# Forward D2 reshuffles on the ScalarE DMA queue, and the row stage's group tables masked by broadcast VectorE products

## The chip, the cores and the metric

One NeuronCore of a Trainium2 chip runs the kernel as one launch. The metric is the device time of a launch in microseconds, the median of several runs. TensorE (PE) multiplies; VectorE (DVE), ScalarE (ACT) and GpSimd (POOL) do elementwise work and move results out of PSUM; SyncE (SP) issues most transfers, and ScalarE can issue transfers too, between its own instructions. Each engine runs its instructions in order, and semaphores join the engines.

## The reference

The kernel computes the output and all gradients of one block in bf16: x is (1, 2048, 448), with S = 2048 and D = 448. A spectral filter is followed by a token-mixing MLP with F = 1792.

```python
def _A_ref(x, w_r, w_i):
    X = rfft2(x.astype(float32), axes=(-2, -1))
    X = X * (w_r + 1j * w_i)
    return irfft2(X, s=(S, D), axes=(-2, -1)).astype(bfloat16)

def _B_ref(x, w1, b1, w2, b2):
    h = _layernorm(x, axis=-1)
    u = _gelu(einsum("bsd,sf->bdf", h, w1) + b1)
    return (einsum("bdf,fs->bds", u, w2) + b2).transpose(0, 2, 1)

h  = x + _A_ref(_layernorm(x), A_w_r, A_w_i)
h2 = h + _B_ref(_layernorm(h), B_w1, B_b1, B_w2, B_b2)
# outputs: h2, and its vjp with grad_out for x, w_r, w_i, w1, b1, w2, b2
```

## The kernel before

The Fourier transforms are done as matrix products with tables that the kernel generates at its start. The transform over S is split in two: a *row stage*, 16 steps of short transforms together with the transform over D, and a *column stage* over 16 groups, with twiddle tables `Ut` and `Vt` of 128 x 16 x 128. Between the two the data changes its layout through eight SBUF-to-SBUF transfers into the tile `D2` (called reshuffles here, R0 to R7, one for each two rows; 226 KB each). The inverse transform goes through another set into `D3`.

**Row stage (lines 905 to 937).** In step t, `row_a(t + 1)` multiplies one folded row block by the table `Rs` (the row's 1/sigma times `Rm`, made on VectorE by `scale_R`), and its PSUM bank is moved to `blks` in `rS`. `row_b(t - 1)` multiplies these blocks by `csF`; its bank goes to `css`, a ring of four buffers. After each odd row, `row_b` puts off by 1.1 us of matmul time a transfer to `D2` (line 693), issued by SyncE. VectorE also makes the folds (`fold_prep`) and the statistics of later rows (`ln_stats`).

**Filler.** `fill(n)` takes n steps of a pending generator, so that TensorE has other products between the small ones. In the row and column stages the generator is `dg_gen`: 14 blocks of 16 matmuls of transposed W2 by grad_out. Each block's 128 x 16 x 128 transpose is a DMA transpose on SyncE (line 297, `load_w2T`) into one of five slots, three in `rE` and two in `rO`; transposes are counted from 0 to 13 here. Eight are loaded during the row stage; from the column stage's start, `fwd_x(0)` interleaves the rest with the loads of the filter's imaginary part (line 583, `w_load`, four transfers for each of the two parts, the first two of 64 and 48 partitions). `w_place` then moves the filter into its place with 16 copies on either engine. Between the last row and the column stage stands `fill(20)`.

**Group tables.** `gen_UV` (line 465) makes `Ut` and `Vt` step by step inside the row stage, up to three steps in each row, where a `yield True` ends the row's share. For each table, ScalarE computes a sine into `comp` (128 x 512), and eight products of its even or odd elements with a mask column (0 or 1 for each partition) are written to strided places of the table, 16 x 16 elements each. Each goes to the engine with the smaller estimated load.

**Who evicts.** `evac` compares two running sums of estimated cost, `load[0]` for ScalarE and `load[1]` for VectorE, and gives the eviction to the one that would be done first. PE, SP, DVE and ACT run in an order that is settled when the program is built; a change of one estimate moves later evictions from one engine to the other.

**DMA semaphores.** In the built program each transfer reports on one of eight semaphores, which are dealt out in turn over the transfers of all engines in the scheduled order. The issuing engine first waits until the previous transfer on that semaphore has landed. The first matmul of the column stage waits for all eight reshuffles.

**Last stage (lines 1407 to 1420).** `inv_rows` runs 16 rows of the inverse transform; each row takes `N_FILL_B[5]` steps of `gw_gen`, the weight-gradient products, whose evictions go to store buffers. `gx_consumer` gives each row to ScalarE, VectorE and GpSimd in small operations, and one of these goes out with each filler step. `drain()` runs what is left of the generator after the last row. `store_4` (line 1328) sends the stores of the filter-gradient of `w1`, and the last two of them from ScalarE's queue, the rest from SyncE's.

Of the kernel before, what the change touches and what calls it, by code (L numbers as in the profile page):

```python
# [10 lines left out]
BF16 = mybir.dt.bfloat16  # L11
F32 = mybir.dt.float32
I32 = mybir.dt.int32
ALU = mybir.AluOpType
ACT = mybir.ActivationFunctionType
AX = mybir.AxisListType

P = 128
# [6 lines left out]
NT = 16  # L25
# [9 lines left out]
RESH_LAG = 1.1  # L35
# [1 line left out]
SIDE = 2  # L37
CAP = 8
N_FILL_F = (6, 3, 20, 3, 24, 2)
N_FILL_B = (16, 16, 40, 8, 24, 8)  # L40
INV_SD = 1.0 / float(S * D)


# [79 lines left out]
def kernel(  # L123
# [20 lines left out]
    nc = tc.nc  # L144
    Ring.held.clear()
    load = [0.0, 0.0]
    sc = Meter(nc.scalar, load, 0)
    ve = Meter(nc.vector, load, 1)
    gp_ = nc.gpsimd
# [5 lines left out]
    mem = ctx.enter_context(tc.tile_pool(name="mem", bufs=1))  # L155
# [15 lines left out]
    def ring(reg, off, count, *dims):  # L171
        n = int(np.prod(dims))
        return Ring([cut(reg, off + i * n, *dims) for i in range(count)])
# [28 lines left out]
    def defer(us, fn, *views):  # L202
        state = [fn]

        def run():
            if state:
                state.pop()()
        later.append((clock[0] + us, len(later), run))
        later.sort(key=lambda x: x[0])
        for v in views:  # L210
            Ring.held.setdefault(id(v), []).append(run)
# [43 lines left out]
    def col(n=1):  # L255
        i = _ci[0]
        _ci[0] += n
        assert _ci[0] <= 64
        return cols[:, i:i + n]
# [145 lines left out]
    def gp_madd(out, in0, scalar, in1):  # L405
        gp_.tensor_scalar(out=gtmp, in0=in0, scalar1=scalar, scalar2=None, op0=ALU.mult)
        gp_.tensor_tensor(out=out, in0=gtmp, in1=in1, op=ALU.add)
# [45 lines left out]
    def masks(eng, c_, f_):  # L453
        msk, mk, k0, k1 = col(4), col(), col(), col()
        for j in range(4):
            eng.tensor_scalar(out=msk[:, j:j + 1], in0=f_, scalar1=float(j), scalar2=None, op0=ALU.is_equal)
        eng.tensor_tensor(out=mk, in0=msk[:, 0:1], in1=c_, op=ALU.mult)
        eng.tensor_scalar(out=k1, in0=mk, scalar1=-1.0, scalar2=1.0, op0=ALU.mult, op1=ALU.add)
        eng.tensor_tensor(out=k0, in0=mk, in1=msk[:, 0:1], op=ALU.subtract)
        eng.tensor_scalar(out=k0, in0=k0, scalar1=1.0, scalar2=None, op0=ALU.add)  # L460
        return msk, mk, k0, k1

    comp_ring = ring(rO, 0, 2, 512)

    def gen_UV():
        _, s_, c_, f_ = rows = decode(gp_)
        nrow = col()
        gp_madd(nrow, rows[0], 16.0, s_)
        msk, mk, k0, k1 = masks(gp_, c_, f_)
        slf = col()  # L470
        gp_.tensor_tensor(out=slf, in0=s_, in1=f_, op=ALU.mult)
        gp_.tensor_scalar(out=slf, in0=slf, scalar1=16.0, scalar2=1536.0, op0=ALU.mult, op1=ALU.add)
        ou, ov0, ov1, pu, pv = col(), col(), col(), col(), col()
        gp_madd(ou, c_, 1536.0, slf)
        gp_madd(ov0, c_, -512.0, slf)
        gp_.tensor_scalar(out=ov0, in0=ov0, scalar1=512.0, scalar2=None, op0=ALU.add)
        gp_.tensor_scalar(out=ov1, in0=ov0, scalar1=1024.0, scalar2=None, op0=ALU.add)
        for pt, o, kk in ((pu, ou, -1536.0), (pv, ov1, -512.0)):
            gp_.tensor_scalar(out=pt, in0=s_, scalar1=64.0, scalar2=kk, op0=ALU.mult, op1=ALU.add)
            gp_madd(pt, pt, mk, o)  # L480
        yield
        ve.tensor_scalar(out=permI[:], in0=krow[:, 0:P], scalar1=nrow, scalar2=None, op0=ALU.is_equal)
        ve.scalar_tensor_tensor(out=base[:, 0, :, 1], in0=fix, scalar=mk, in1=base[:, 0, :, 1], op0=ALU.mult, op1=ALU.add)
        for dst, o0, o1, pt in ((Ut, ou, ou, pu), (Vt, ov0, ov1, pv)):
            t = ftmp(1024 if dst is Ut else 2048, 16, 16, 2).bitcast(I32)
            for k, o in ((0, o0), (1, o1)):
                ve.tensor_scalar(out=t[:, :, :, k], in0=base[:, :, :, k], scalar1=s_, scalar2=o,
                                 op0=ALU.mult, op1=ALU.add)
                yield
            ve.tensor_scalar(out=t[:, 0, :, 1], in0=base[:, 0, :, 1], scalar1=s_, scalar2=pt, op0=ALU.mult, op1=ALU.add)  # L490
            ve.tensor_scalar(out=t, in0=t, scalar1=2047, scalar2=None, op0=ALU.bitwise_and)
            yield
            yield True
            comp = comp_ring.next()
            sc.activation(out=comp, in_=t.rearrange("p g l c -> p (g l c)"), func=ACT.Sin, scale=s2048, bias=half_uv)
            yield True
            cv = comp.rearrange("p (g l c) -> p g l c", g=16, l=16)
            for c, k in ((1, k0), (0, k1)):
                ve.tensor_scalar(out=cv[:, 0, :, c], in0=cv[:, 0, :, c], scalar1=k, scalar2=None, op0=ALU.mult)
            yield  # L500
            d0 = dst[:, :, 0:64].rearrange("p g (l f) -> p g l f", f=4)
            d1 = dst[:, :, 64:112].rearrange("p g (l f) -> p g l f", f=3)
            for j in range(4):
                m = msk[:, j:j + 1]
                dj = d1[:, :, :, j - 1] if j else dst[:, :, 112:128]
                for o, c in ((d0[:, :, :, j], 0), (dj, 1)):
                    if load[1] + 0.24 < load[0] + 0.38:
                        ve.tensor_scalar(out=o, in0=cv[:, :, :, c], scalar1=m, scalar2=None, op0=ALU.mult)
                    else:
                        sc.activation(out=o, in_=cv[:, :, :, c], func=ACT.Copy, scale=m)  # L510
                    yield
    Rp = rO[:, 1536:1536 + P]

    def gen_RT():
# [87 lines left out]
    D2 = cut(r2, 0, NG, 2, KW)  # L602
# [4 lines left out]

    _ei = [0]

    def resh_eng():  # L610
        _ei[0] += 1
        return nc.sync

    def rowbase(s_):
        return 32 * (s_ // 4) + s_ % 4
# [54 lines left out]
    def row_b(h, quarters=False):  # L670
        u, c = divmod(h, 2)
        if u < 0 or u >= NT // 2:
            return
        pd = ps_ff()
        pv = pd[:, 0:452].rearrange("p (c k) -> p c k", c=2)
        pq = pd[:, 0:452].rearrange("p (c e k) -> p c e k", c=2, e=2)
        for w in (1, 0):
            for b in range(2):
                if quarters:
                    mm(pq[:, 1 - w, b, :], lhsT=blks[u][0:DC, 2 * (2 * w + b) + c].rearrange('p j x -> p (j x)'),  # L680
                       rhs=csB[0:DC, w, b, 0:KW // 2], start=True, stop=True)
                    continue
                mm(pv[:, 1 - w, :], lhsT=blks[u][0:DC, 2 * (2 * w + b) + c].rearrange('p j x -> p (j x)'), rhs=csF[0:DC, w, b, :],
                   start=(b == 0), stop=(b == 1))
        if c == 0:
            css[u] = cs_ring.next()
        cs = css[u]
        if quarters:
            evac(out=cs[:, c].rearrange("p w (j e) -> p w e j", e=2), in_=pq)
        else:  # L690
            evac(out=cs[:, c], in_=pv)
        if c:
            defer(RESH_LAG, lambda: nc.sync.dma_start(out=D2[u:u + 121:8].rearrange("p g c k -> p (g c k)"),
                                                      in_=cs.rearrange("p x c k -> p (x c k)")), cs)

    def s2_stage(get_x, on_mult, ml, n_fill, gap, make_inv, after_fwd=None, scale=None):
# [203 lines left out]
    for c in range(2):  # L900
        sc.copy(out=Rp.rearrange("p (a q b c) -> p c a q b", c=2, q=8, a=4)[:, c],
                in_=Rm[:, 64 * c:64 * c + 64].rearrange("p (q a b) -> p a q b", q=8, a=4))
    FILL_A = (3, 3, 3, 3, 3, 3, 3, 3, 3, 3, 3, 3, 3, 3, 3, 3)
    FILL_B = (3, 3, 3, 3, 3, 3, 3, 3, 3, 3, 3, 3, 3, 3, 3, 3)
    for t in range(NT):
# [11 lines left out]
        if t == NT - 1:  # L917
            row_b(t)
# [7 lines left out]
        if t in GROUPS:  # L926
            a, b = GROUPS[t]
# [232 lines left out]
    for ch in range(2):  # L1160
        ve.tensor_scalar(out=csI[0:KC, :, ch, :], in0=csI[0:KC, :, ch, :], scalar1=halves[0:KC, ch:ch + 1], scalar2=None,
                         op0=ALU.mult)
# [120 lines left out]
    o4 = out_4.rearrange("(p t) f -> p t f", t=NT)  # L1283
# [41 lines left out]
                            out(pv, w, c + 1, i)  # L1325
                        yield

    def store_4(t, a, n, o):
        eng = nc.scalar if t >= NT - 2 and a else nc.sync
        eng.dma_start(out=o4[:, t, a:a + n], in_=o[:, 0:n])  # L1330

    pending.append(gw_gen(NFB, lambda c, k, a, b: goT[a:b, k, c * 512:(c + 1) * 512], S,
                          lambda j, a, n, o: nc.sync.dma_start(out=out_6[j * P:(j + 1) * P, a:a + n], in_=o[:, 0:n]), ost))
    pending.append(gw_gen(NT, lambda c, k, a, b: du_t[c][a:b, :, k, :], F,
                          store_4,
                          Ring(ring(rG, 0, 8, S // 2).views + ost.views), NFB // 2))
    load_W(3)
    for t in range(NT - LAG, NT + 2):
# [9 lines left out]
    for i in range(2):  # L1348
        gen_neg(UTn[:, 8 * i:8 * i + 8, :], UTt[:, 8 * i:8 * i + 8, :])
    fill(N_FILL_B[2])  # L1350
    Meter.slack = 4.0
    s2_stage(bwd_x, bwd_mult, 0, N_FILL_B[3], N_FILL_B[4], False, {5: lambda: load_du(0), 9: lambda: load_du(1), 13: lambda: load_du(2)}, 2.0 * INV_SD)
    Meter.slack = 2.0
# [57 lines left out]

    inv_rows(gx_consumer, N_FILL_B[5], aT_ring, (), True)
    while held_ops:
# [36 lines left out]
```

## Time and profile before

| | |
|---|---|
| runs | 359.11, 358.55, 359.77 us (median 359.11) |
| profiled execution | 359.11 us, its span 357.2 us |
| busy of the span: PE, ACT, DVE, POOL | 96%, 60%, 71%, 19% |
| transfers: bytes moved, mean rate | 81.62 MB, 229 GB/s |
| granted TensorE clock, mean | 0.987 |

The span is the time from the first to the last instruction that the profiler saw; the launch's own time is 1.9 us longer. Times below count from the start of the span. The busy share of TensorE is that of pipelined matmuls whose ends are modelled, so a full slice says that TensorE was not waiting, and no more. The chain that ended last is mostly TensorE's own:

```profile
PE 79%; ACT 7%; DVE 6%; DMA 4%; issue 2%; SPq 1%; POOL 0%; ACTq 0%; DVEq 0%
PE ps_mm L218 66%; PE ps_ff L218 13%; DMA rO<-in_B_w_dram 2%; ACT rO L82 2%; DVE stats L82 2%; ACT rG L82 1%; DMA rA<-in_A_x_dram 1%; DVE r L82 1%; ACT Ut L82 1%; DVE rA L82 1%; DVE rS L82 1%; SPq L297 1%; ACT Vt L82 1%; ACT rX L82 0%; ACT rS L82 0%
```

Nearly all elementwise work has line 82 and nearly all matmuls line 218, since helpers record them; tiles tell them apart: `rS` holds the row stage's blocks, `r` several buffers (`css` and `D2` among them), `rX` the column stage's results.

### The profile page before, as it was taken

How to read it: one execution, taken by the hardware profiler on the slowest of the kernel's cores; microseconds unless marked ns; L12 is line 12 of the kernel's file. 1: busy time of each engine (PE TensorE's matmuls, PEld its weight loads, DVE VectorE, ACT ScalarE, POOL GpSimd, SP SyncE). 2: the span in 40 equal slices, each digit the busy share in tenths (PEclk: the TensorE clock that was granted, in tenths of full speed). 3: DMA queues.
4: the chain of work that ended last, by engine and by line, in shares of the span. 5: the costliest groups of instructions: out<-in, count | busy, mean ns of one | idle time of the engine just before them, and what ended most of it. 6: DMA issues, size and time to landing. Idle time of an engine off the chain costs nothing.

```text
span 357.2 us, 6450 instructions
## 1 busy us (share of the span) xinstructions
PE 341.5 (96%) x2133; PEld 183.8 (51%) x2133; DVE 252.5 (71%) x679; ACT 213.8 (60%) x457; POOL 67.7 (19%) x227
## 2 busy tenths in 40 slices
PE   6898998899999999999999999999999999999994
PEld 2455665555645555555555555544444444455641
DVE  5897626992884888775226978784498766499994
ACT  4669836965986545504221355565477776588883
POOL 8667000000220000001001111110000000056771
PEclk9699999999999999999999999999999999999998
DMA  8999999847999999997886999999976878999996
GB/s 207 287 200 234 200 198 162 169 140 252 280 292 336 302 348 241 252 246 218 194 192 134 192 210 194 221 175 264 264 214 201 238 196 236 245 215 221 247 286 234
DMA packets 147672, 81.62 MB, mean 229 GB/s; under 512 B 95480, under 2 KB 139768, under 8 KB 147384
## 3 DMA queue, kind: packets, MB, share of 16 engines
q1 hardware_dynamic: 147352, 80.83, 94.7%
q8 instruction: 16, 0.26, 0.3%
q10 hardware_dynamic: 288, 0.39, 0.3%
q14 instruction: 16, 0.13, 0.1%
HBM read 27.56 MB, written 23.89 MB: 144 GB/s over the span
## 4 chain that ended last, share of the span: by engine, by line
PE 79%; ACT 7%; DVE 6%; DMA 4%; issue 2%; SPq 1%; POOL 0%; ACTq 0%; DVEq 0%
PE ps_mm L218 66%; PE ps_ff L218 13%; DMA rO<-in_B_w_dram 2%; ACT rO L82 2%; DVE stats L82 2%; ACT rG L82 1%; DMA rA<-in_A_x_dram 1%; DVE r L82 1%; ACT Ut L82 1%; DVE rA L82 1%; DVE rS L82 1%; SPq L297 1%; ACT Vt L82 1%; ACT rX L82 0%; ACT rS L82 0%
## 5 line engine op out<-in xcount | busy, mean ns | idle before, releaser
L218 PEld LDWEIGHTS <-r 128*128 128x128 bf16 (+2 forms) x660 | 61.7, 104 | 49.6 <-issue 2.7
L218 PEld LDWEIGHTS <-rS 128*128 128x128 bf16 (+2 forms) x496 | 40.5, 99 | 38.3 <-issue 7.0
L218 PE MATMUL ps_mm<-rD,r 128*128 128x448 bf16 x224 | 44.5, 352 | 0.0
L82 ACT CAST rO<-ps_mm 128x512 bf16<-128x512 f32 (+1 forms) x62 | 33.5, 583 | 13.8 <-PE ps_mm L218 11.1
L218 PE MATMUL ps_mm<-rC,rE 128*128 128x448 bf16 x144 | 36.0, 369 | 3.3 <-DMA rC<-in_grad_out_dram 3.3
L218 PEld LDWEIGHTS <-rst 128*128 128x128 bf16 (+1 forms) x320 | 23.8, 97 | 29.3 <-issue 13.5
L82 ACT CAST r<-ps_ff 128x452 bf16<-128x452 f32 x58 | 33.4, 576 | 8.8 <-PE ps_ff L218 8.4
L218 PE MATMUL ps_mm<-r,rst 128*128 128x512 bf16 (+3 forms) x192 | 36.4, 353 | 0.0
L218 PE MATMUL ps_mm<-rB,r 128*128 128x448 bf16 x160 | 31.2, 352 | 0.1
L218 PE MATMUL ps_mm<-rG,rst 128*128 128x512 bf16 (+1 forms) x128 | 28.2, 380 | 0.0
L82 ACT ACTIVATE r<-ps_mm,rstd_h 128x448 bf16<-128x448 f32 x16 | 10.1, 633 | 26.1 <-PE ps_mm L218 26.1
L82 ACT ACTIVATE r<-rC 128x448 bf16<-128x448 bf16 x16 | 9.1, 572 | 26.8 <-DMA out_dram<-r 12.9
L82 DVE SCALAR_TENSOR_TENSOR r<-ps_mm,b2col,r 128x448 bf16<-128x448 f32 x16 | 10.9, 682 | 19.9 <-PE ps_mm L218 17.9
L82 DVE CAST rO<-ps_mm 128x512 bf16<-128x512 f32 (+1 forms) x18 | 11.8, 658 | 15.2 <-PE ps_mm L218 14.3
L82 ACT ACTIVATE rG<-rG 128x896 bf16<-128x896 bf16 x14 | 13.3, 950 | 14.9 <-DVE rG L82 14.6
L218 PEld LDWEIGHTS <-rO 128*128 128x128 bf16 (+1 forms) x165 | 15.6, 98 | 12.2 <-DMA rO<-in_B_w_dram 1.8
L218 PE MATMUL ps_mm<-rE,rS 128*128 128x448 bf16 x112 | 21.5, 352 | 0.0
L82 ACT CAST rG<-ps_mm 128x512 bf16<-128x512 f32 (+1 forms) x33 | 16.6, 541 | 7.3 <-PE ps_mm L218 7.2
L1180 POOL TENSOR_SCALAR lcol<-lcol 128x1 f32<-128x1 f32 x16 | 8.5, 530 | 65.1 <-ACT r L82 65.1
L218 PE MATMUL ps_mm<-rC,rO 128*128 128x448 bf16 x80 | 19.1, 352 | 1.5 <-DMA rO<-in_B_w_dram 1.5
L1371 POOL TENSOR_SCALAR lcol<-lcol 128x1 f32<-128x1 f32 x16 | 5.5, 342 | 78.5 <-ACT r L82 78.5
L218 PEld LDWEIGHTS <-rE 128*128 128x128 bf16 x148 | 14.4, 101 | 11.3 <-issue 5.0
(198 smaller groups left out, 662.6 us busy)
## 6 DMA issues: line engine op xcount, KB each, us to landing
out_dram<-rO SPq DMA_DIRECT2D x34, 256.0 KB
r<-in_B_w_dram SPq DMA_DIRECT2D x5, 1024.0 KB
r<-r SPq DMA_DIRECT2D x16, 226.0 KB
r<-r SPq DMA_DIRECT2D x32, 113.0 KB
rS<-in_B_w_dram SPq DMA_DIRECT2D x4, 896.0 KB
out_dram<-rG SPq DMA_DIRECT2D x10, 256.0 KB
rO<-in_B_w_dram SPq DMA_DIRECT2D x2, 1024.0 KB
w_d<-rG SPq DMA_DIRECT2D x1, 1808.0 KB
```

The costliest lines, as they stand in the source:

```text
L82: fn(**kw)
L218: nc.tensor.matmul(out, lhsT=lhsT, rhs=rhs, start=start, stop=stop)
L297: nc.sync.dma_start_transpose(out=wT, in_=B_w2[j * P:(j + 1) * P, :].rearrange("f (t c) -> f t c", c=P))
L1180: gp_.tensor_scalar(out=m1, in0=ms, scalar1=-1.0 / D, scalar2=None, op0=ALU.mult)
L1371: gp_.tensor_scalar(out=m1, in0=ms, scalar1=-2.0 / D, scalar2=None, op0=ALU.mult)
```

## The change

Four things differ.

1. The reshuffles of the forward pass are issued by ScalarE. The backward pass (`quarters`) keeps SyncE. At each issue 0.55 us is added to ScalarE's estimated load.
2. In `gen_UV`, seven of the eight mask products of each table become two products on VectorE: one of 16 x 16 x 4 and one of 16 x 16 x 3 elements a partition, whose second operand is the mask row in bf16 (`mskb`, copied once by GpSimd), repeated over groups and lanes, while the first operand repeats each sine over the masks. Each ends the row's share of `gen_UV` (`yield True`). The eighth goes to either engine by the load sums (`evac_mask`).
3. The last stage takes 9 filler steps in each row, not 8.
4. All stores of the filter gradient leave from SyncE's queue.

```diff
-N_FILL_B = (16, 16, 40, 8, 24, 8)
+N_FILL_B = (16, 16, 40, 8, 24, 9)
...
+    mskb = mem.tile([P, 1, 1, 4], BF16, name="mskb")
+
+    def evac_mask(out, in_, m):
+        if load[1] + 0.43 < load[0] + 0.7:
+            ve.tensor_scalar(out=out, in0=in_, scalar1=m, scalar2=None, op0=ALU.mult)
+        else:
+            load[0] += 0.3
+            sc.activation(out=out, in_=in_, func=ACT.Copy, scale=m)
...
         msk, mk, k0, k1 = masks(gp_, c_, f_)
+        gp_.tensor_copy(out=mskb[:, 0, 0, :], in_=msk)
...
-            for j in range(4):
-                m = msk[:, j:j + 1]
-                dj = d1[:, :, :, j - 1] if j else dst[:, :, 112:128]
-                for o, c in ((d0[:, :, :, j], 0), (dj, 1)):
-                    if load[1] + 0.24 < load[0] + 0.38:
-                        ve.tensor_scalar(out=o, in0=cv[:, :, :, c], scalar1=m, scalar2=None, op0=ALU.mult)
-                    else:
-                        sc.activation(out=o, in_=cv[:, :, :, c], func=ACT.Copy, scale=m)
-                    yield
+            for out, c, j in ((d0, 0, 0), (d1, 1, 1)):
+                n = 4 - j
+                load[1] += 0.06 + 256.0 * n / 960.0
+                nc.vector.tensor_tensor(out=out, in0=cv[:, :, :, c:c + 1].broadcast_to([P, 16, 16, n]),
+                                        in1=mskb[:, 0:1, 0:1, j:4].broadcast_to([P, 16, 16, n]), op=ALU.mult)
+                yield True
+            evac_mask(dst[:, :, 112:128], cv[:, :, :, 1], msk[:, 0:1])
+            yield
...
-    def resh_eng():
-        _ei[0] += 1
-        return nc.sync
+    def resh_eng(on_act=True):
+        if not on_act:
+            return nc.sync
+        load[0] += 0.55
+        return nc.scalar
...
-            defer(RESH_LAG, lambda: nc.sync.dma_start(out=D2[u:u + 121:8].rearrange("p g c k -> p (g c k)"),
+            defer(RESH_LAG, lambda: resh_eng(not quarters).dma_start(out=D2[u:u + 121:8].rearrange("p g c k -> p (g c k)"),
                                                       in_=cs.rearrange("p x c k -> p (x c k)")), cs)
...
-    def store_4(t, a, n, o):
-        eng = nc.scalar if t >= NT - 2 and a else nc.sync
-        eng.dma_start(out=o4[:, t, a:a + n], in_=o[:, 0:n])
-
...
-                          store_4,
+                          lambda t, a, n, o: nc.sync.dma_start(out=o4[:, t, a:a + n], in_=o[:, 0:n]),
```

In the program that the changed kernel builds to, the loads of the filter and the transposes follow each other on SyncE without the reshuffles between them, and the eight semaphores are dealt out anew: R0 to R7 share theirs with, in this order, transpose 1, the last load of x, the load of b1, transpose 5, R2, R3, R4 and the first load of the imaginary filter.

## The prediction

> **What bounds the kernel now.** I read the slices first, then the waits of TensorE, then the queues in the stretch where they fall. The two rows below are TensorE's busy tenths and the mean share of the 16 DMA engines, in 40 slices of 8.9 us.
>
> ```profile
> PE   6898998899999999999999999999999999999994
> DMA  8999999847999999997886999999976878999996
> ```
>
> TensorE is full from slice 13 (107 us) to the tail, so only the first 105 us and the last 7 hold time to win; there the DMA engines are as full. The list of TensorE's waits (total, times, longest) has three of weight:
>
> ```profile
> PE ps_ff L218 <- ACT rS L82: 1.6, 1, 1.6
> PE ps_mm L218 <- DMA rO<-in_B_w_dram: 1.5, 1, 1.5
> PE ps_ff L218 <- ACT rX L82: 0.9, 1, 0.9
> ```
>
> The timeline puts them at 28.4, 59.15 and 67.7 us. The first is the row stage: ScalarE works on the group tables while row 7's bank, complete at 26.1, waits for its eviction.
>
> ```profile
> 27.64 1.93 ACT L82 ACTIVATE Ut<-rO,cols 128x256 bf16<-128x256 bf16 x3
> 29.30 0.69 ACT L82 CAST rS<-ps_ff 128x512 bf16<-128x512 f32 x1
> ```
>
> The second is a late W2 transpose, number 9 of 14 (counted from 0). SyncE's queue shows why:
>
> ```profile
> 37.62 1.05 SPq L583 DMA_DIRECT2D rB<-in_A_w_r_dram  x2
> 41.59 5.57 SPq L693 DMA_DIRECT2D r<-r  x3
> 47.25 2.24 SPq L297 DMA_TRANSPOSE rO<-in_B_w_dram  x1
> 49.55 2.35 SPq L583 DMA_DIRECT2D rB<-in_A_w_i_dram  x4
> 52.00 5.02 SPq L297 DMA_TRANSPOSE rO<-in_B_w_dram  x1
> ```
>
> From 38.7 to 47.2 SyncE stands before the last three D2 reshuffles, which wait for evictions, and transpose 8, the four loads of the imaginary filter and transpose 9 stand behind them. The trace's semaphore updates give the landings: reshuffles R0 to R7 at 31.50, 34.51, 38.06, 39.27, 45.08, 47.94, 48.67, 50.01; transpose 8 at 51.95; the first imaginary load (64 partitions) at 54.58; transpose 9 at 60.61. The column stage's first matmul, which needs all of D2, starts at 50.31, without a stall but only 0.3 us after R7.
>
> How much those reshuffles held up shows in the DMA share, the column after the granted clock:
>
> ```profile
> 27.00:41.00 14.00, 12.38 (x103) 8.27 (x102) 10.35 (x35) 12.67 (x25) 6.72 (x30) 1.00 1.13 233
> 41.00:47.00 6.00, 5.96 (x48) 4.08 (x47) 3.39 (x8) 3.63 (x8) 0.11 (x1) 1.00 0.97 154
> 47.00:50.00 3.00, 3.00 (x18) 1.56 (x16) 0.23 (x1) 0.53 (x1) 0.00 (x0) 1.00 0.64 139
> ```
>
> Saturated, the engines read 1.13; before R7 lands they have slack.
>
> **The masks.** Sixteen products go, 11 on ScalarE and 5 on VectorE; in come four broadcast products on VectorE (128x1024 and 128x768 twice) and two 128x256 products, which the order of the changed program puts on ScalarE.
>
> ```profile
> L82 ACT ACTIVATE Ut<-rO,cols 128x256 bf16<-128x256 bf16 x6 | 3.9, 771 | 0.5 <-DVE rO L82 0.5
> L82 DVE TENSOR_SCALAR Vt<-rO,cols 128x256 bf16<-128x256 bf16 x3 | 1.0, 451 | 0.0
> ```
>
> ScalarE: 3.9 + 3.0 (the Vt group) = 6.9 us for 11, 0.63 each in a run; 9 fewer are 5.6 us less. VectorE: three strided products took 0.99 us end to end, 0.33 each for 256 columns, so 1024 cost at most 4 x 0.33 = 1.32 and 768 0.99. The dense 128x904 product, 0.624 us, is the other bound: 0.71 and 0.53. Operands and output are strided here, so I take near the upper end, 1.15 and 0.9: 4.1 us for both tables, less 5 x 0.33 = 1.65 gone, +2.5 us. Laid into VectorE's row from 25.6 us (rescale, fold, statistics in order), they finish the fold for rows 8 and 9 at 27.5, when row 8 starts (27.48), and the fold for rows 10 and 11 0.1 to 0.2 us late. Row 7's eviction moves from 29.3 to about 26.9. So this part takes 1.3 to 1.6 us off the row stage. [...]
>
> **The reshuffles.** Eight issues move from SyncE (0.53 to 0.70 us each) to ScalarE, +4.5 us there against 5.6 gone. Each also waits: every transfer reports on one of eight semaphores dealt out in turn over both queues, and waits until the previous user has landed. In the changed program R7 takes the semaphore of the first imaginary load: ScalarE may not issue R7 before that load lands. In the kernel before its predecessor was R3, landed at 39.27. Behind R7 on ScalarE stand the eviction of transpose 6's product and the column stage's evictions; TensorE's first column matmul waits for R7 itself.
>
> So: when does that load land? SyncE, freed, issues transposes 6 and 7, the four real loads, transpose 8 (free once block 3 is consumed, 34.3) and the load at about 37.5, but the engines are full. Counted from 54.58 where it landed before: R6 and R7 no longer go ahead of it, 2 x 1.25 (the spacing of R1 after transpose 6, 1.22, and of R2 after transpose 7, 1.27) = 2.5; the slack is filled, 6 x (1 - 0.97/1.13) + 3 x (1 - 0.64/1.13) = 0.85 + 1.3 = 2.15. That gives 49.9; without the slack 52.1; with the idle 0.6 us at 25 to 26 (share 0.41) filled as well 49.3. R7 would be ready at 45.2 to 46.6. It loses 3 to 5 us.
>
> From the start of its issue R7 took 3.38 us before (46.63 to 50.01). Bounds: 1.94 for a store on an idle queue (351.47 to 353.41), 8.1 for R4 behind two filter loads. On its own queue I take 3.4: landing at 53.3, first column matmul 0.3 later, 53.6 against 50.31: **+3.3 us**. TensorE has nothing but the 20 fill matmuls (4.35 us) to cover this, and those cover R7's old latency. The row stage's 1.5 us vanish into the same wait: it ends by a DMA, not by TensorE.
>
> In return transpose 9, issued about 43.5 and behind some 6 us of loads after 49.9, lands near 57; it is wanted 9.1 us after the column stage starts, at 62.7. Its **1.5 us** wait goes. The 0.9 us wait for the rX eviction stays: ScalarE's order there still has three, then two filter placements (0.95 us each) ahead of it, and two more earlier. Bounds on this: 0.9 won, 0.9 lost.
>
> [...] If R7's 1.3 us of transfer then take turns with the filter loads, it lands 1.3 us later and the sum grows by that; if the own queue is as good as an empty one, the sum is as above.
>
> **The tail.** The fill per row goes from 8 to 9 in the last stage: 16 yields, some 18 matmuls, leave the drain of 46 (7.94 us). TensorE's total is unchanged and it is full from 250 to 345, so its end stays. VectorE needs 2.17 us a row; the row pitch grows from about 2.27 to 2.45, so it stops lagging, but its last row comes 16 x 0.2 = 3.2 us later and ends near 352.7 (was 351.44). The last two stores on SyncE instead of ScalarE: before, the four last ones were issued at 351.90 to 352.90 and landed at 355.79, with the DMA share at 1.0 from 352.5 to 355; bytes decide, not the issuer. After, two of the four no longer stand behind the last out_1 store. I take 0, bounds -0.5 and +0.6.
>
> **Sum.** 359.11 (the profiled execution, which is also the median; span 357.2) + 3.3 - 1.5 = **360.9 us**. With landing 49.3 to 52.1, flight 1.94 to 5 and the tail, it runs from 358.4 to 364; its own likely range is 359.9 to 362.7.
>
> **Rivals.** (a) The wait on the semaphore is short: the load lands by 46, or R7 is later than I think. Then TensorE keeps 1.4 of the row stage and the 1.5: 359.1 - 2.9 = **356.2**, faster. For it: two queues may keep the engines busier than one. Against it: 4.6 us of transfers (transpose 8, the load: 50.01 to 54.58) that ran after R7 now run before it, on engines at 1.13. It decides if R7 lands before about 49. (b) The gate costs what it frees: R7 lands at 51.5 to 52, **359.1**, within 0.3% (about what this kernel's measurement can tell from no change). For it: the slack could be larger than the share says. (c) R7, sharing with filter loads, takes as long as R4, 8.1 us: column stage at 58.3, +8 - 1.5, **365.6**. Against: R4 stood behind those loads in one queue. (d) VectorE, 98% busy from 20 to 30, becomes the row stage's bound; hidden behind the gate if there is one, else (a) loses 0.3 to 1.
>
> **Chances.** Forecast 0.62, (a) with (d) 0.14, (b) 0.18, (c) 0.06. Faster by over 0.3% 0.14, same 0.18, slower 0.68. The range, 358.3 to 363.3, reaches over (b) and leaves out (c) and most of (a).
>
> **What would show it.** After: no wait of TensorE on an rS eviction near 28; ScalarE standing before its last reshuffle from about 46 to 50; a TensorE wait of some 4 us ahead of the first Vt matmul against D2, ended by a DMA; no wait for rO near 60; VectorE's broadcast products 1.1 and 0.9 us long; the last row product later and the last store landing as far after TensorE's end as before (3.6 us). If TensorE enters the column stage before 50, the gate was not there and I am wrong in sign.

## The result, and the profile after

The changed kernel takes 371.09 us (median of 4 runs, 370.57 to 374.07) against 359.12 for the kernel before on the same chip: 1.035 times as long, 95% interval 1.0292 to 1.0408. The forecast was 360.9 us in a range of 358.3 to 363.3. The sign was right and the place was right, but the loss is 12.0 us where 1.8 were expected.

The slices of the page show the place. TensorE, the granted clock, and the mean share of the DMA engines:

```profile
PE   5897960989999999999999999999999999999994
PEclk9798995799999999999999999999999999999998
DMA  8999999633699999999686999997967669999996
```

The span is now 371.9 us, so a slice is 9.3 us long. Counted from 0, slice 5 (46.5 to 55.8 us) is six tenths busy and slice 6 is empty, just where the column stage used to begin; the clock is low in slices 6 and 7. The list of TensorE's waits (total, times, longest) has one new row that carries nearly everything:

```profile
PE ps_ff L218 <- DMA rO<-in_B_w_dram: 12.0, 1, 12.0
PE ps_mm L218 <- DMA rO<-in_B_w_dram: 2.3, 1, 2.3
PE ps_ff L218 <- ACT rX L82: 1.2, 1, 1.2
```

The first row is the wait before the first matmul against `D2`, which starts at 64.65 us (50.31 before). The profile puts it down to the transfer that ended last by its records, a W2 transpose into `rO`; the matmul needs the last reshuffle R7, which landed at 64.52. The second row is another wait, in the row stage: it ends at 30.19, with the landing of transpose 3 at 30.14, and e8, a second profile of the same kernel, does not have it. The row stage's wait for the rS eviction is gone, as forecast, and so is the wait near 60 for transpose 9. ScalarE's timeline (start, us, engine, line, operation) shows where R7 stood:

```profile
49.54 8.52 ACTq L704 DMA_DIRECT2D r<-r  x2
58.09 0.53 ACT L82 CAST rD<-ps_mm 128x448 bf16<-128x448 f32 x1 [10.80 <-DMA rB<-in_A_w_i_dram]
```

R6 and R7 are issued in this group: R6 at 49.54, right after R4, whose semaphore it shares, had landed at 49.46, and R7 only at 57.51, right after the first imaginary load landed at 57.44. And SyncE, which used to stand before R5 to R7, has run ahead:

```profile
38.19 2.47 SPq L592 DMA_DIRECT2D rB<-in_A_w_r_dram  x4
40.76 8.35 SPq L297 DMA_TRANSPOSE rO<-in_B_w_dram  x1
49.16 2.86 SPq L592 DMA_DIRECT2D rB<-in_A_w_i_dram  x4
52.12 8.94 SPq L297 DMA_TRANSPOSE rO<-in_B_w_dram  x1
```

The issue of transposes 8 and 9 and of the imaginary loads begins before R7's. Transpose 8 took 2.24 us to issue before and takes 8.35 now, transpose 9 took 5.02 and takes 8.94; why, no run here isolates. From 14.3 us at the column stage's start to the end little changes: TensorE's last matmul ends 14.6 us later than before (366.82 against 352.21), the span 14.7.

The profiled run (374.07) was the longest of its four. In e8 the column stage starts at 59.34; the sizes of single terms are read from it.

### The profile page after: what moved, and what is told of

The parts are those of the page before. It is cut to its first block, busy times and chain, and to the rows that moved or that the text cites. A ratio compares the mean times of both kernels' runs of the same rounds, so it can differ in the third digit from the quotient of the medians.

```text
span 371.9 us, 6446 instructions
## 1 busy us (share of the span) xinstructions
PE 343.6 (92%) x2133; PEld 184.9 (50%) x2133; DVE 255.0 (69%) x675; ACT 211.3 (57%) x451; POOL 66.9 (18%) x228
## 4 chain that ended last, share of the span: by engine, by line
PE 76%; DMA 7%; DVE 6%; ACT 5%; issue 2%; SPq 1%; POOL 0%; ACTq 0%; DVEq 0%
PE ps_mm L218 63%; PE ps_ff L218 13%; DMA rO<-in_B_w_dram 6%; DVE r L82 3%; ACT rO L82 2%; ACT rG L82 1%; DMA rA<-in_A_x_dram 1%; DVE stats L82 1%; SPq L297 1%; DVE rA L82 1%; ACT r L82 0%; ACT rX L82 0%; DVE rG L82 0%; DVE rX L82 0%; DVE rS L82 0%
## 5 line engine op out<-in xcount | busy, mean ns | idle before, releaser
L218 PE MATMUL ps_mm<-rC,rE 128*128 128x448 bf16 x144 | 37.5, 379 | 3.2 <-DMA rC<-in_grad_out_dram 2.3
L82 ACT CAST r<-ps_ff 128x452 bf16<-128x452 f32 x56 | 32.3, 577 | 11.5 <-PE ps_ff L218 11.3
L218 PE MATMUL ps_ff<-r,Vt 128*128 128x452 bf16 x32 | 11.8, 367 | 13.2 <-DMA rO<-in_B_w_dram 12.0
L218 PE MATMUL ps_mm<-rC,rO 128*128 128x448 bf16 x80 | 20.1, 370 | 2.3 <-DMA rO<-in_B_w_dram 2.3
L82 DVE CAST rO<-ps_mm 128x512 bf16<-128x512 f32 x17 | 11.6, 689 | 15.3 <-PE ps_mm L218 14.5
L82 ACT ACTIVATE rG<-rG 128x896 bf16<-128x896 bf16 x14 | 13.3, 950 | 14.9 <-DVE rG L82 14.7
L218 PEld LDWEIGHTS <-rE 128*128 128x128 bf16 x148 | 14.5, 103 | 12.3 <-issue 5.1
L1191 POOL TENSOR_SCALAR lcol<-lcol 128x1 f32<-128x1 f32 x16 | 8.5, 531 | 65.1 <-ACT r L82 65.1
```

The lines of the kernel that those rows point to most:

```text
L82: fn(**kw)
L218: nc.tensor.matmul(out, lhsT=lhsT, rhs=rhs, start=start, stop=stop)
L1191: gp_.tensor_scalar(out=m1, in0=ms, scalar1=-1.0 / D, scalar2=None, op0=ALU.mult)
```

## The experiments

The candidates after the first profile were: A, two queues in flight at once slow each other; B (later G), the semaphore that R7 shares with the first imaginary load is a gate and the gate is the loss; C, the other parts carry some of it. Theory O, that what matters is only what has been issued ahead of the reshuffles, came out of e9 below. Each ratio is to runs of the kernel before made together with that experiment (medians from 359.12 to 360.25 us).

**e1: the reshuffles back on SyncE, all else of the change kept.**

```
-resh_eng(not quarters).dma_start(out=D2[...
+resh_eng(False).dma_start(out=D2[...
```

> The changed kernel with its eight forward D2 reshuffles back on SyncE's queue; masks by broadcast products, the fill of 9 and the two stores on SyncE stay. Theory A (two queues in flight at once slow each other's transfers) and theory B (only the shared-semaphore gate of the last reshuffle costs) both say that all of the +12 us goes with the queue: first column matmul at 48.7 to 50.3 us, the TensorE wait on the rS eviction near 28 gone, transpose 9 as late as before (1.5 us): 357.5 to 359.3 us. Theory C (the masks, the fill or the stores carry a good part of it) says 363 or more.

Measured 359.06 us, 0.9998 [0.9982, 1.0014] of before. C falls: masks, fill and stores together are worth nothing that can be told. The first column matmul starts at 49.74, 0.57 earlier than before.

**e2: the reshuffles on ScalarE, nothing else changed from before.**

```
-    nc.sync.dma_start(out=D2[...
+    (nc.sync if quarters else resh_eng()).dma_start(out=D2[...
...
     def resh_eng():
-        _ei[0] += 1
-        return nc.sync
+        load[0] += 0.55
+        return nc.scalar
```

> The kernel before with nothing changed but the queue: the eight forward reshuffles leave from ScalarE. The last reshuffle again has the first imaginary load as its predecessor on the semaphore. Theory A: first column matmul at 62 to 66 us, transposes of SyncE 5 to 9 us each to issue, 369 to 373 us. Theory B: the gate is there but the load lands near 50 to 52 without the masks' help, 360 to 364 us. Theory C: 359 to 361 us.

Measured 366.71, 1.0212 [1.0185, 1.0238]: the queue alone loses 7.6 us, between the expectations of A and B. The first imaginary load landed at 52.61, R7 was issued at 52.71 and landed at 58.42; column stage from 58.55. The gate is there, and R7's flight of 5.7 us comes on top.

**e5: the imaginary loads asked for one step later, so R7 follows R3 on its semaphore.**

```
-            for kind in "TWWWWTTT":
+            for kind in "TTTT":
...
+        if c2 == 1:
+            for _ in range(4):
+                next(w_loads)
```

> The changed kernel with the four imaginary-filter loads asked for one step of the column stage later, so that transposes 9 to 13 go ahead of them on SyncE and the last reshuffle's predecessor on its semaphore becomes reshuffle R3 (landed at 41.7 in the changed kernel). Theory A: flights stay at 6 to 12 us, R6 and R7 land at 55 to 60, first column matmul there, 364 to 368 us. Theory B (the gate alone): first column matmul at 50 to 52, 358 to 361 us.

Measured 368.06, 1.0261 [1.0215, 1.0308]. R7 was issued at 46.15 and the column stage began at 53.28, 11 us before the first profile of the changed kernel but still 3.0 after the kernel before: R7 took 6.9 us and landed 0.2 us before transpose 9, which SyncE had issued ahead of it. The time is not won. The span of e5 is 7.6 us longer than before: 3.0 are this start, some 2.7 the half clock that follows the idle time before it (5.4 us of it), 3.3 more us of waits for rX (4.2 for 0.9; the imaginary loads now land at 64 to 68), less the 1.5 us wait for transpose 9, which goes.

**e7 and e11: R7 alone moved, to SyncE and to ScalarE.**

```
e7:  +resh_eng(not quarters and u != 7).dma_start(out=D2[...
e11: +resh_eng(not quarters and u == 7).dma_start(out=D2[...
```

> The changed kernel with one reshuffle of eight, the last (R7), back on SyncE's queue. On its semaphore R7 then follows the first real-filter load, landed long before; SyncE again stands before R7 and issues transpose 8 and the imaginary loads behind it. Theory B (the gate: what costs is R7 held until the imaginary load has landed): nearly all of the +12 us goes, first column matmul at 50 to 52, 358 to 361 us. Theory A (copies of a second queue and SyncE's transposes slow each other): R0 to R6 still take 6 to 12 us, R6 lands after 54, first column matmul at 55 or later, 363 us or more.

> The mirror image: only R7 leaves from ScalarE, R0 to R6 from SyncE. Its predecessor on the semaphore is the first real-filter load, so there is no gate, but transpose 8 and the imaginary loads are issued by SyncE without waiting for R7 and share the engines with it. Theory B: R7 is issued at 46 to 47 as before, lands at 50 to 53, first column matmul there, 357 to 361 us. Theory A: R7's flight grows to 6 us or more, first column matmul at 53 to 56, 361 to 364 us.

e7: 358.97, 0.9994 [0.9965, 1.0022], column stage at 49.97. Seven of eight reshuffles on the second queue cost nothing, so A in its plain form falls. e11: 361.0, 1.001 [0.9981, 1.0038]; no gate, but transpose 8 was issued (44.51) before R7 (46.17), R7 took 6.0 us, and the column stage began at 52.24, 1.9 late. The time hardly shows it, because transpose 9 is then no longer waited for (1.5 us).

**e8: the changed kernel again.**

> The changed kernel once more, for a second profile, since the first one was of a run 3 us above the others. If the late stretch of the first profile (transpose 7 landing at 42.6, R3 at 41.7) belongs to that run alone, the first column matmul is at 60 to 62 and the time at 370.5 to 371.5; if it belongs to the kernel, it stays at 64 to 65.

Measured 370.94 in the profiled run and 367.91, on average 9.3 over the kernel before of the same group. The column stage starts at 59.34, so 5 us of the first profile's 64.65 belong to that run. The stretches of e8 (length, then busy time and instructions of TensorE, its weight loads, VectorE, ScalarE and GpSimd; then granted clock, DMA share, GB/s):

```profile
40.00:50.00 10.00, 9.98 (x73) 6.31 (x73) 4.97 (x11) 2.27 (x4) 0.11 (x1) 1.00 1.13 177
50.00:59.30 9.30, 0.00 (x0) 0.00 (x0) 0.00 (x0) 1.02 (x2) 0.00 (x0) 0.74 1.15 186
59.30:62.00 2.70, 2.66 (x10) 1.41 (x11) 0.63 (x1) 0.00 (x0) 0.00 (x0) 0.50 1.07 231
62.00:65.00 3.00, 3.00 (x17) 1.91 (x16) 0.63 (x1) 1.82 (x6) 0.11 (x1) 0.54 0.44 99
```

TensorE does nothing for 9.3 us while the DMA share reads 1.15, and the column stage then begins at half clock.

**e9: the reshuffles on GpSimd's queue, which shares no semaphore with SyncE's transfers.**

```
+(nc.sync if quarters else nc.gpsimd).dma_start(out=D2[...
```

> The changed kernel with the eight reshuffles on GpSimd's queue in place of ScalarE's: no reshuffle shares a semaphore with SyncE's transfers, so no gate, but again two queues in flight at once, and SyncE runs ahead to the imaginary loads. Theory B: first column matmul at 50 to 54, 358 to 363 us (GpSimd's own issue time is not known from any row and may add to it). Theory A: flights of 6 to 12 us stay, first column matmul at 56 to 62, 364 to 370 us.

Measured 368.69, 1.0233 [1.0176, 1.0289], column stage at 59.56. Without any gate R7 left at 48.22 and landed at 59.43, 11.2 us later and 0.2 us before transpose 9 (59.62). B fails here. Either GpSimd's queue is slow by itself, or what SyncE had put on the engines stands in front of the reshuffles whatever their own queue is: theory O.

**e12: all reshuffles on ScalarE, but SyncE held.** A 32-byte copy on SyncE reads R7's buffer, so SyncE stands before it until R7's data is there.

```
+            if u == 7 and not quarters:
+                defer(RESH_LAG, lambda: nc.sync.dma_start(out=hold, in_=cs[0:1, 1, 1, 0:16]), cs)
```

> The changed kernel, all eight reshuffles on ScalarE's queue, with one 32-byte copy added on SyncE that reads the last reshuffle's buffer: SyncE stands before it until that buffer is evicted, as it stood before R5 to R7 in the kernel before, and issues transpose 8 and the imaginary loads only then. On its semaphore R7 then follows the first real-filter load. Theory O (what costs is that SyncE, freed, runs ahead and its transpose 8, imaginary loads and transpose 9 stand in front of the reshuffles on the shared engines): first column matmul at 49.5 to 51.5, 358 to 360.5 us. Theory A (reshuffles on a second queue are slow in themselves): R4 to R7 take 6 us or more, first column matmul at 54 or later, 363 us or more.

SyncE's timeline of e12; `hold` is the small copy:

```profile
45.77 0.57 SPq L708 DMA_DIRECT2D hold<-r  x1
46.44 2.52 SPq L297 DMA_TRANSPOSE rO<-in_B_w_dram  x1
49.02 2.32 SPq L593 DMA_DIRECT2D rB<-in_A_w_i_dram  x4
```

R7, issued on ScalarE at 45.77, lands at 49.61 (3.8 us), and the column stage starts at 49.74, as in e1, with all eight on the second queue. In this profile (a run of 359.83) the whole loss is gone. Its ten runs spread from 359.2 to 365.1, for a reason that this profile doesn't show: their median is 362.95, above the 358 to 360.5 that O expected, and the ratio 1.0036 [0.9999, 1.0073] is that of the seven shortest, without three of 364.8 to 365.1. So e12 shows the cause by its times of landing and start; as a cure it is less sure than e7.

**e3 and e4: after and before with plain copies in place of the transposes.** Transposes were suspected (theory T), since reshuffles kept landing 0.1 to 0.3 us before one. Each W2 block is copied untransposed in 256-byte pieces; what is computed from it is not the reference's.

```
-        nc.sync.dma_start_transpose(out=wT, in_=B_w2[j * P:(j + 1) * P, :].rearrange("f (t c) -> f t c", c=P))
+        rows = B_w2[j * P:(j + 1) * P, :].rearrange("f (t c) -> (f t) c", c=P)
+        nc.sync.dma_start(out=wT, in_=rows.rearrange("(t p) c -> p t c", p=P))
```

> The changed kernel with its 14 W2 transposes replaced by plain copies of the same bytes in 256-byte pieces (the filter-gradient inputs come out untransposed, so part of the output is not the reference's). To be read against e4_before_plain. Theory T (a reshuffle of the second queue lands only as the transpose in flight on SyncE's queue ends, 0.1 to 0.3 us before it, and this is a property of transposes): without transposes R0 to R6 take 2 to 4 us, and e3 stands 2 to 6 us over e4. Theory O (any bytes issued ahead have the same effect): flights of 4 to 10 us stay, and e3 stands 8 to 12 us over e4.

> The kernel before with the same replacement of its 14 transposes by plain copies. Under every theory the order on SyncE's one queue stays, so 357 to 361 us if such copies move as fast as transposes; it is the base for e3_after_plain.

e4: 358.25, 0.9937 [0.9916, 0.9959]; e3: 372.72, 1.035 [1.0292, 1.0408], 14.5 us over e4, with the column stage at 62.00 against 48.88. In e3 the reshuffles R4 to R7 take 7.6 to 10.3 us from issue to landing, where T expected 2 to 4 of R0 to R6, so the loss does not need transposes. The gap of 14.5 us is larger than the 8 to 12 that was expected of O, and cannot be read as O's alone, because another gate is in it: R4 shares its semaphore with a real-filter load that landed at 43.48, and ScalarE stood before R4 until then, with evictions behind it (ScalarE's timeline, then TensorE's wait for them):

```profile
43.58 0.54 ACTq L705 DMA_DIRECT2D r<-r  x1
44.16 0.54 ACT L82 CAST r<-ps_ff 128x452 bf16<-128x452 f32 x1 [9.71 <-DMA rB<-in_A_w_r_dram]
```

```profile
PE ps_ff L218 <- ACT r L82: 8.0, 1, 8.0
```

**e13: e1 with transpose 9 asked for before the imaginary loads.**

```
-            for kind in "TWWWWTTT":
+            for kind in "TTWWWWTT":
```

> e1_resh_sync (masks by broadcast, everything on SyncE's queue) with transpose 9 asked for before the four imaginary loads in place of after them. If order on the shared engines is what sets these times, transpose 9 lands at 55 to 56 in place of 60.4, TensorE's wait for it (1.9 us in e1) goes, and the imaginary loads land some 2.5 us later (60), which the filter placements may or may not feel: 357.0 to 358.0 us if not, 358.5 to 359.5 if so.

Measured 359.38 where before took 360.21 over the runs it is compared with: 0.9969 [0.9943, 0.9994]. Transpose 9 lands at 54.61, TensorE no longer waits for it, the imaginary loads end at 60.29 (57.45 in e1). It has the lowest ratio of the kernels that compute the reference, but 0.3% is about what can be told from nothing and 1.9 us of wait won are hardly seen in the time.

**e6 and e15: gate and bytes apart.** In e6 the smallest imaginary piece goes out before transpose 8; this turns the semaphores by one, so that R7 follows R4 and R6 follows transpose 8. R7 then has no gate of its own, but it stands behind R6 on ScalarE, and R6 waits for transpose 8. In e15 (one queue, like e1) transpose 8, the imaginary loads and transpose 9 are asked for before R6 and R7.

```
e6:  +        for c_, d, ps in ((0, A_w_r, parts), (1, A_w_i, parts[3:]), (1, A_w_i, parts[:3])):
     +        for _ in range((9, 10, 11, 12, 12).count(t)):
     +            for kind in "TWWWTTT":
...
e15: +        if t == 13:
     +            for kind in "TWWWWT":
...
     +            for kind in "TT":
```

> The changed kernel with the smallest piece of the imaginary filter (16 partitions of 225 numbers) asked for before transpose 8 in place of last. This turns the semaphores by one: R7 follows R4, R6 follows transpose 8, R5 the last real-filter piece; none follows an imaginary load of any size. All reshuffles stay on ScalarE and SyncE runs ahead as in the changed kernel. Theory G (the semaphore of the imaginary load holds R7, and that wait is the loss): R7 can leave when transpose 8 has landed, 50 to 51.5, takes 3.4 and the first column matmul is at 54 to 55.5, 362 to 365 us. Theory O (the bytes that SyncE has issued ahead are the loss, with or without the semaphore): R7 lands with transpose 9, first column matmul at 58 to 60, 367 to 371 us.

> e1_resh_sync (masks by broadcast, everything on SyncE's queue, 359.06) with transpose 8, the four imaginary loads and transpose 9 asked for before R6 and R7 in place of after them: no second queue, and no reshuffle on the semaphore of a load that is still under way. Theory O: the same bytes stand ahead of R6 and R7, so R7 lands at 55 to 60 and the column stage starts there: 362 to 369 us. Theory A or G (the second queue itself, or its semaphore): neither is there, so 358.5 to 361 us.

e6: 371.07, 1.0295 [1.0226, 1.0363]. R6 left at 50.28, after transpose 8 had landed at 50.20; R7 left at 50.93, its own semaphore free since 49.27, and landed at 59.49, 8.6 us later; column stage at 59.63, where the gated kernel has 59.34. A gate of the kind seen in e3 costs TensorE 2.6 us of the row stage here (R4, held until transpose 7 landed at 40.14), so the time of e6 is not that of a kernel without gates; R7's landing is what it tells. e15: 369.91, 1.0264 [1.0213, 1.0315], with neither a second queue nor such a semaphore. SyncE's timeline of e15, the reshuffles last but one:

```profile
40.41 7.63 SPq L297 DMA_TRANSPOSE rO<-in_B_w_dram  x1
48.10 2.35 SPq L592 DMA_DIRECT2D rB<-in_A_w_i_dram  x4
50.55 5.00 SPq L297 DMA_TRANSPOSE rO<-in_B_w_dram  x1
55.65 1.27 SPq L704 DMA_DIRECT2D r<-r  x2
57.02 5.54 SPq L297 DMA_TRANSPOSE rE<-in_B_w_dram  x2
```

and the row of its TensorE waits (total, times, longest):

```profile
PE ps_ff L218 <- issue: 10.2, 1, 10.2
```

R7 lands at 59.86 and the column stage starts at 60.07. The profile names no releaser for this wait, but the first matmul starts 0.2 us after R7's landing; in the other runs of the table below it is 0.04 to 0.2.

The column stage's start thus follows one thing, what SyncE has issued ahead of R7:

| kernel | ahead of R7 | R7 issued, landed | column stage | ratio to before |
|---|---|---|---|---|
| e12 (ScalarE, SyncE held) | nothing new | 45.77, 49.61 | 49.74 | 1.0036 |
| e7 (R7 on SyncE) | nothing new | 46.18, 49.83 | 49.97 | 0.9994 |
| e11 (R7 on ScalarE) | transpose 8 | 46.17, 52.20 | 52.24 | 1.001 |
| e5 (no gate) | transposes 8, 9 | 46.15, 53.08 | 53.28 | 1.0261 |
| e8 (gate) | transposes 8, 9, imaginary loads | 53.60, 59.20 | 59.34 | 1.0268 |
| e6 (R7 behind R6, no gate of its own) | the same | 50.93, 59.49 | 59.63 | 1.0295 |
| e9 (GpSimd, no gate) | the same | 48.22, 59.43 | 59.56 | 1.0233 |
| e15 (one queue) | the same | 56.36, 59.86 | 60.07 | 1.0264 |

The last four differ in queue and gate, leave R7 over a range of 8 us, and land it within 0.7. e2, with the old masks, is like e8: 52.71, 58.42 and 58.55. The ratios of e5 and e6 hold other losses too, as said above, and that of e12 leaves out its three longest runs.

## Why the prediction was right in sign and wrong in size

**The masks.** Right in the products and in the wait, too high in the gain. The broadcast products took 1.22 and 0.93 us for 1.15 and 0.9 (VectorE's timeline of the changed kernel):

```profile
25.45 1.22 DVE L516 TENSOR_TENSOR Ut<-rO,mskb 128x1024 bf16<-128x1024 bf16 x1
28.11 0.93 DVE L516 TENSOR_TENSOR Ut<-rO,mskb 128x768 bf16<-128x768 bf16 x1
```

The 1.6 us wait for the rS eviction went, and the gain vanished before the column stage. e1 shows how small it is even without the second queue: where 1.3 to 1.6 us were forecast for the row stage, R7 is issued 0.84 us earlier (45.79 for 46.63), lands 0.40 earlier, and transpose 9's wait takes 0.4 back:

```profile
PE ps_mm L218 <- DMA rO<-in_B_w_dram: 1.9, 1, 1.9
```

**The gate.** Its existence, place and order were right: R7 left 0.07 us after the first imaginary load landed (0.08 in e8). But the forecast made it the cause, and e6 and e9 show that it is only another form of the wait: without it R7 leaves 2.7 us (e6) and 5.4 us (e9) sooner than in e8 and lands 0.2 to 0.3 later. The forecast also priced this one gate alone: R6 waited for R4 (issued at 45.53 in e8, R4 landed at 45.45), for which its sum has no term.

**The failing step: the load's landing, 49.9 us.** In e8 it was 53.52, 3.6 late and beyond the bounds of 49.3 to 52.1. The forecast took 54.58 and drew 2.15 us from "the slack is filled", reading the DMA share as a rate: 1.13 full, 0.97 and 0.64 free. The share is the time that packets were under way, not bytes: it reads 1.13 at 233 GB/s in the forecast's own first row and 1.15 at 186 in e8. The kernel before, over the same stretch as e8's first row above:

```profile
40.00:50.00 10.00, 9.96 (x73) 6.26 (x71) 4.52 (x11) 5.17 (x11) 0.11 (x1) 1.00 0.90 157
```

157 GB/s x 10 us are 1.57 MB, against 1.77 MB in e8. A share a quarter higher moved 0.20 MB more, 1.1 us at the 186 GB/s of the next stretch. The other 2.5 us, for R6 and R7 no longer standing ahead of it, are not there in full either: the load lands 1.1 earlier than before for both terms together, in e8 (53.52) as in e15 (53.45), where both reshuffles come after it on one queue.

**The second failing term: R7's flight, 3.4 us "on its own queue".** It was 5.6 in e8 (7.0 in the first profile), and 8.6 in e6. The queue was its own, the way was not: transpose 9, whose issue ran from 47.56 to 56.13 in e8, landed at 59.45, 0.25 after R7. R7 did not move slowly, it waited. These are the packets, MB and share by queue from 53.95 to 57.4 us and from 57.4 to 58.3 in e8; q1 is SyncE's queue and q10 ScalarE's, whose one packet in the first stretch has 4 bytes:

```profile
q1 hardware_dynamic: 1968, 0.58, 121.5%
q10 hardware_dynamic: 1, 0.00, 0.1%
```

```profile
q10 hardware_dynamic: 144, 0.23, 83.6%
q1 hardware_dynamic: 188, 0.04, 31.3%
```

The whole of R7 passes in 0.8 us, from 3.9 us after its issue on. A transpose is 2048 packets of 256 bytes here, so the trace lets one count when its last packet starts: 57.45 for transpose 9 in e8, and R7's first packet starts at 57.45. It is 56.67 and 56.67 in e2, 62.87 and 62.88 in the first profile, 50.34 and 50.34 for transpose 8 and R7 in e11, and in e6 56.58 for transpose 9 and for R6, which R7 follows. In these five cases the reshuffle on ScalarE's queue thus went when the transpose that SyncE had begun ahead of it was through, and no earlier; whether it stood at the engines or before them, the trace does not tell.

The forecast had this transpose in its sum, but only as a gain for TensorE later, and not as bytes in front of R7; rival (c), R7 as slow as R4 behind loads, was set aside because "R4 stood behind those loads in one queue". e15 and e6 show that one queue or two makes no difference there.

That transfers of two queues stand in each other's way is what the runs show (the column stage starts at 59.34 in e8, on two queues, and at 60.07 in e15, on one), and the forecast, which weighed it at 1.3 us, should have let it decide. That the queues take turns, on which that 1.3 us rested, was the author's assumption. In the five cases just shown ScalarE's queue took none. Elsewhere there are some: R5's packets start from 49.87 to 54.05 in the first profile, among those of transpose 8, whose last starts at 53.87, and on GpSimd's queue in e9 R7's run from 54.76 to 58.73, where transpose 9's last starts at 57.94, and it still lands at 59.43. Nor is the late landing a matter of what comes after the packets: R7 lands 0.95 us after its last packet ends in e8 (58.25, 59.20) and 0.99 in e12 (48.62, 49.61), where it lands early.

**The rivals.** (a) fell: R7 did not land before 49. What (b) described, a late start paid for by transpose 9's wait, is e11: +1.9 and -1.5. (d) was small: in e1 TensorE's waits for VectorE between 20 and 75 us are 0.8 us in all, where they were 0.5.

**The clock, a term that was missing.** After the idle stretch of e8 the clock is 0.50 for 2.7 us and 0.54 for 3.0. TensorE's work went by it: on the chain that ended last three filler matmuls take 1.12 us at 60.25 and 0.57 at 65.83. That makes an estimate of 2.7 x 0.50 + 3.0 x 0.46 = 2.7 us.

**The sum again.** In e8: start of the column stage +9.0 (3.6 + 2.2 more than the +3.3 forecast), clock +2.7, transpose 9's wait gone -1.5, makes +10.2; the last matmul with `Vt` of the backward pass's column stage indeed starts 10.2 later (302.39 for 292.15). The tail, taken as 0 with bounds of -0.5 and +0.6, is at the upper bound or over it: the last store lands 3.58 us after TensorE's last matmul before, 4.18 in the changed kernel, 4.25 in e1, 5.23 in e8. With it the span of e8 is 11.7 longer (TensorE's end 10.5). In e1 it eats what the masks brought: TensorE ends 0.3 us earlier, the span 0.1.

e2 loses 7.6 us and the full change 12.0 (9.3 in e8's two runs), though their column stages start at 58.55 and 59.34. Of the 3.7 us between the spans of the two profiles, 365.2 and 368.9, the tail makes 1.6 (3.59 against 5.23), the start 0.8 and the shorter half clock some 0.6 (4.3 us against 5.4); the rest was not taken apart.

Two things stay open. Of the 5.3 us by which the first profile was later than e8 at the column stage's start, 2.7 are there when the row stage ends, after the wait at 30.19 and the half clock that followed it; from 22 to 30 us the transfers ran at 108 GB/s there and at 213 in e8, and why is not shown. And the spread of e12 has no cause shown.

## What to carry to other kernels

An engine that stands before a late transfer is also holding back everything queued behind it, as SyncE did in the kernel before until 47.2 us. Before moving that transfer to another queue, list what the first queue will issue instead, and price the moved transfer as landing after what has been issued ahead of it, whatever queue it is on (here R7 landed at 59.20 to 59.86 from three different queues). If the transfer is urgent, keep the hold (leave the last urgent transfer on the busy queue, as in e7, or make the queue wait for its data, as in e12, whose times spread), and read free DMA capacity from bytes, not from the busy share (1.13 stood beside 177 GB/s in e8 and beside 233 in the kernel before).

## What the runs showed of the hardware

TensorE's granted clock was halved after idle stretches far shorter than the long waits, but not after each of them. After an idle of 2.2 us (e11) the granted clock stayed at 1.00; after 3.8 us (e5) it was 0.50 at the restart. These are the first stretches of the column stage in each:

```profile
52.20:54.00 1.80, 1.76 (x12) 1.12 (x13) 0.63 (x1) 0.21 (x1) 0.00 (x0) 1.00 1.29 252
```

```profile
53.20:55.00 1.80, 1.72 (x6) 0.88 (x7) 0.63 (x1) 0.00 (x0) 0.00 (x0) 0.50 1.21 274
```

The same 1.8 us hold 12 matmuls in e11 and 6 in e5. But the half clock also followed an idle of 2.35 us in the first profile's row stage, and one of 2.6 in e6's (two filler matmuls take 0.89 us there at 43.76, three take 0.73 from 45.10 on); these are four cases and no rule. In the first profile the clock fell 1.4 us after the restart and was back 3.4 us later:

```profile
27.84:30.19 2.35, 0.00 (x1) 0.00 (x1) 2.35 (x8) 0.88 (x2) 1.94 (x5) 1.00 1.30 129
30.19:31.60 1.41, 1.41 (x10) 0.94 (x11) 1.41 (x6) 0.24 (x1) 1.14 (x4) 1.00 1.23 330
31.60:35.00 3.40, 3.40 (x16) 1.94 (x15) 1.32 (x7) 1.50 (x4) 2.60 (x11) 0.50 1.21 219
35.00:37.00 2.00, 2.00 (x18) 1.33 (x17) 0.47 (x1) 1.41 (x3) 1.41 (x8) 0.99 1.03 229
```

The half clock there lasted 3.4 us, longer than the idle before it. At the column stage the clock was full again 4.3 us after the restart in e2 (which had waited 5.6 us), 4.5 in the first profile (12.0), and 5.4 in e8 (9.4) and in e5 (3.8).

What a semaphore gate cost here depended on what stood behind it. A transfer released 5 us sooner landed no sooner (e8 and e9: issued at 53.60 and 48.22, landed at 59.20 and 59.43), so there the gate itself cost nothing that can be seen. Where evictions stood behind the gate on ScalarE, TensorE stopped for them: 8.0 us in e3, 2.6 us in e6.
